# A static order for every engine, LN transposes by DMA and a denser attention: two layers of local attention and FFN on one core

## The chip, the cores and the metric

One core of one Trainium2 chip. The time is the device time of one execution in microseconds (us), as the median of several executions. The program runs on one core, so there is no second die to compare with; all runs told here are in the fast state. Each ratio is to runs of the kernel before on the same chip in the same rounds. Differences between two versions ("above the changed kernel") cross rounds and chips; the kernel before had medians of 1329.9 to 1330.6 us in them, so a microsecond between two versions is not read as a gain or a loss.

## The reference, cut to what matters

```python
# x: (1, 2048, 1024) bf16; 32 heads of 32; window 8, dilation 2; FFN width 3584
def _A_ref(x, wqkv, wo):
    q, k, v = ...                       # x @ wqkv, per head
    idx = pos[:, None] - (jnp.arange(8) * 2)[None, :]
    logits = einsum("bhsd,bhswd->bhsw", q, k[idx]) * scale   # masked where idx < 0
    o = einsum("bhsw,bhswd->bhsd", softmax(logits), v[idx])
    return o.reshape(B, S, D) @ wo

def _B_ref(x, w1, b1, w2, b2):
    r = relu(x @ w1 + b1)
    return (r * r) @ w2 + b2

x = A_x
for _ in range(2):                      # written out twice in the reference
    x = x + _A_ref(_layernorm(x), A_wqkv, A_wo)
    x = x + _B_ref(_layernorm(x), B_w1, B_b1, B_w2, B_b2)
```

## The kernel before

The work is cut into 8 units (2 layers x 4 blocks of 512 rows). A unit has these stages: SA (layernorm of the input and its transposition to channels on partitions), SQ (the q, k and v projections: `pq`), S2 (local attention, mostly on DVE), SW (the output projection `py`, residual, second layernorm and transposition), SF (the FFN: `ph` up, `py` down). Generators for the stages are advanced in turn so that a unit's attention runs on DVE while TensorE (PE) does another unit's FFN; a scheduler then orders the instructions by automatic priorities.

A layernormed tile of 128 rows is transposed by eight PE transposes through PSUM:

```python
def ln_transpose(self, xt, xnT, tl, dve_stats=False, evac_act=False):
    xn = self.xp.tile([128, D], BF, name="xn", tag="xn")          # pool of 2
    # ... mean and variance by two ACT passes over the tile (bn_stats on DVE where dve_stats)
    nc.scalar.activation(out=xn[:], in_=xt, func=ACTF.Identity, bias=nmr[:], scale=rstd[:])
    pt = self.ps_t.tile([128, self.KD, 128], BF, name="pt", tag="pt")
    for kd in range(self.KD):
        nc.tensor.transpose(pt[:, kd, :], xn[:, kd * 128:(kd + 1) * 128], self.ident[:])
    # ... copied to xnT by DVE or ACT
```

Attention: products `P` on DVE, summed in a tree of depth 2; a matmul of 32 columns for each window position gives logits by rows; softmax there; probabilities are transposed back by PE (`ptp`) and weight the values on DVE.

```python
for w in range(W):                                                # logits: lg
    for i, Pp in enumerate(d["finals"]):
        nc.tensor.matmul(lg[:, tl2, w, :], Pp[:, w, tl2*128:(tl2+1)*128], self.ind[:], ...)
# ... max, subtract, exp, sum, reciprocal, multiply
for w in range(W):                                                # back: ptp
    nc.tensor.transpose(ptp[:, w, :], p4[:, tl2, w].rearrange("p h r -> p (h r)"), self.ident[:])
# ... for every c: multiply with the v window, then three adds (8 -> 4 -> 2 -> 1 positions)
```

The order of the stages and the weights that are loaded ahead follow one list:

```python
for u in range(NU):
    if u + 1 < NU: prim.append(('SQa', u + 1))      # k, q
    prim.append(('SW', u))
    if u + 1 < NU: prim.append(('SQb', u + 1))      # v
    prim.append(('SF', u))                          # in two halves of the FFN width
```

## Time and profile before

| | before |
|---|---|
| time, median of the first 4 runs (of all 12) | 1330.5 us (1330.6) |
| span of the profiled run, granted clock | 1328.5 us, 0.996 |
| first `pq`; first `ph` | 16.93; 135.45 us |
| steady period of a unit | 161.1 us |
| DMA | 223.69 MB, 168 GB/s |

The page, the steady period and its matmuls are shown in the prediction. What it tells of the end in words only is PE's timeline where the last unit's SW stands alone. Columns here and in all timelines: start and duration in us, engine, line, operation, output<-inputs, shapes, count, and in brackets the idle time before it and what ended it.

```profile
1203.36 7.50 PE L457 MATMUL py<-wt,oT 128*128 128x512 bf16 x33
...
1217.48 0.62 PE L193 MATMUL pt<-ident,xn 128*128 128x128 bf16 x8 [0.20 <-ACT xn L190]
...
1221.44 0.62 PE L193 MATMUL pt<-ident,xn 128*128 128x128 bf16 x8 [2.91 <-ACT xn L190]
1224.70 1.03 PE L193 MATMUL pt<-ident,xn 128*128 128x128 bf16 x8 [2.64 <-ACT xn L190]
1226.56 8.61 PE L485 MATMUL ph<-xnT,wt 128*128 128x512 bf16 x31 [0.82 <-DVE xnT L198]
```

The reader is to see that from 1203.36 to 1226.56 PE has only this stage to do, that it waits for the layernorm result `xn`, 2.91 and 2.64 us for the last two tiles, and that the up projection cannot begin before the last tile is transposed.

### The profile page before, as it was taken

What the parts mean: (1) busy time and instruction counts of PE and PEld (TensorE: products, weight loads), DVE (VectorE), ACT (ScalarE), POOL (GpSimd) and SP (SyncE); (2) the same over time, 40 slices, a digit from 0 to 9 for tenths busy, and PEclk for the clock granted to TensorE, in tenths of its full rate; (3) what the DMA queues carried; (4) which work ended last, traced back from release to release, by engine and by line L of the source; (5) the groups of instructions that cost most, each with busy time, mean ns of one, the idle gap of its engine ahead of it and who ended that gap; (6) DMA issues with size and microseconds to landing.
All of it is one profiled execution on the core that took longest, in us unless ns stands there. A gap on an engine that the chain in (4) does not pass through costs nothing.

```text
span 1328.5 us, 17261 instructions
## 1 busy us (share of the span) xinstructions
PE 1285.2 (97%) x6972; PEld 679.8 (51%) x7104; DVE 830.1 (62%) x1170; ACT 681.1 (51%) x1229; POOL 2.9 (0%) x9
## 2 busy tenths in 40 slices
PE   6999999999999999999999999999999999997998
PEld 3665444654446544455445554455544555443443
DVE  4599993394935949268582777719676197926011
ACT  4647826287342964239561494615836166142622
POOL 0000000000000000000000000000000000000000
PEclk9999999999999999999999999999999999999999
DMA  8435544646355554656456464456644564446341
GB/s 214 160 127 158 175 141 146 205 159 201 126 196 185 180 175 143 200 189 206 123 174 235 160 221 152 135 188 212 200 127 163 195 214 131 130 150 223 127 135 56
DMA packets 180847, 223.69 MB, mean 168 GB/s; under 512 B 8608, under 2 KB 143776, under 8 KB 180768
## 3 DMA queue, kind: packets, MB, share of 16 engines
q1 hardware_dynamic: 177168, 222.58, 50.8%
q0 software_dynamic: 3600, 0.01, 0.4%
q8 instruction: 55, 0.90, 0.3%
q14 instruction: 24, 0.20, 0.0%
HBM read 209.98 MB, written 12.58 MB: 168 GB/s over the span
## 4 chain that ended last, share of the span: by engine, by line
PE 73%; DVE 14%; ACT 11%; issue 1%; DMA 0%; SPq 0%; ACTq 0%
PE py L506 29%; PE ph L485 28%; PE pq L268 12%; DVE P L316 5%; DVE P L335 4%; ACT xn L190 3%; ACT xn L181 3%; ACT xn L185 2%; PE pt L193 1%; DVE pr L411 1%; PE py L457 1%; PE ptp L398 1%; DVE xm L459 1%; ACT vT L270 1%; PE lg L362 1%
## 5 line engine op out<-in xcount | busy, mean ns | idle before, releaser
L485 PE MATMUL ph<-xnT,wt 128*128 128x512 bf16 x1751 | 393.2, 380 | 3.0 <-DVE xnT L198 0.8
L506 PE MATMUL py<-wt,r2t 128*128 128x512 bf16 x1753 | 389.4, 379 | 2.1
L268 PE MATMUL pq<-xnT,wt 128*128 128x512 bf16 x1500 | 341.0, 381 | 3.0 <-DVE xnT L198 0.8
L506 PEld LDWEIGHTS <-r2t 128*128 128x128 bf16 x1792 | 174.5, 98 | 207.1 <-ACT r2t L490 0.4
L485 PEld LDWEIGHTS <-wt 128*128 128x128 bf16 x1792 | 174.2, 98 | 206.7 <-issue 3.1
L268 PEld LDWEIGHTS <-wt 128*128 128x128 bf16 x1536 | 216.8, 144 | 107.5 <-issue 3.7
L489 ACT ACTIVATE r<-ph,b1T 128x512 bf16<-128x512 f32 x224 | 152.9, 683 | 98.3 <-PE ph L485 96.9
L411 DVE TENSOR_TENSOR pr<-pb,vT 128x2048 bf16<-128x2048 bf16 x128 | 156.1, 1235 | 44.2 <-ACT pb L399 44.2
L316 DVE TENSOR_TENSOR P<-qT,kT 128x2048 bf16<-128x2048 bf16 x128 | 153.7, 1226 | 37.0 <-ACT qT L270 37.0
L490 ACT ACTIVATE r2t<-r 128x512 bf16<-128x512 bf16 x224 | 140.7, 629 | 5.5
L270 ACT CAST kT<-pq 128x512 bf16<-128x512 f32 x64 | 37.6, 587 | 189.3 <-PE pq L268 189.3
L457 PE MATMUL py<-wt,oT 128*128 128x512 bf16 x496 | 114.0, 383 | 0.8
L335 DVE TENSOR_TENSOR P<-P 128x2048 bf16<-128x2048 bf16 x84 | 102.5, 1221 | 0.4
L412 DVE TENSOR_TENSOR pr<-pr 128x1024 bf16<-128x1024 bf16 x128 | 87.4, 698 | 0.0
L516 DVE TENSOR_TENSOR xo<-py,xm 128x512 bf16<-128x512 f32 x32 | 22.1, 692 | 101.9 <-PE py L506 100.0
L399 ACT COPY pb<-ptp 128x1024 bf16<-128x1024 bf16 x32 | 31.6, 1013 | 104.1 <-PE ptp L398 103.9
L457 PEld LDWEIGHTS <-oT 128*128 128x128 bf16 x512 | 50.1, 99 | 59.0 <-issue 2.4
L512 DVE TENSOR_TENSOR xm<-py,xm 128x512 f32<-128x512 f32 x64 | 44.4, 693 | 52.2 <-PE py L506 49.4
L270 ACT CAST qT<-pq 128x512 bf16<-128x512 f32 x64 | 37.5, 586 | 65.3 <-PE pq L268 65.3
L193 PE MATMUL pt<-ident,xn 128*128 128x128 bf16 x512 | 41.5, 227 | 29.5 <-ACT xn L190 28.7
L521 DVE TENSOR_TENSOR xof<-py,xm 128x512 f32<-128x512 f32 x32 | 22.1, 692 | 76.5 <-PE py L506 59.5
L193 PEld LDWEIGHTS <-xn 128*128 128x128 bf16 x512 | 32.4, 101 | 51.4 <-ACT xn L190 45.5
(61 smaller groups left out, 737.4 us busy)
## 6 DMA issues: line engine op xcount, KB each, us to landing
wt<-in_B_w_dram SPq DMA_DIRECT2D x88, 1024.0 KB, 6.0
wt<-in_A_wqkv_dram SPq DMA_DIRECT2D x48, 1024.0 KB, 6.0
wt<-in_B_w_dram SPq DMA_DIRECT2D x32, 768.0 KB, 4.5
wt<-in_A_wo_dram SPq DMA_DIRECT2D x16, 1024.0 KB, 6.2
xt<-xs SPq DMA_DIRECT2D x32, 512.0 KB, 4.4
xt<-in_A_x_dram SPq DMA_DIRECT2D x32, 256.0 KB, 3.7
xs<-xof SPq DMA_DIRECT2D x32, 256.0 KB, 3.1
out_dram<-xo SPq DMA_DIRECT2D x32, 128.0 KB, 2.0
```

What stands on the lines that cost most here:

```text
L193: nc.tensor.transpose(pt[:, kd, :], xn[:, kd * 128:(kd + 1) * 128], self.ident[:])
L268: nc.tensor.matmul(pq[:], fetch(nm)[kd // 4][:, kd % 4, c0:D:8], xnT[:, kd, :], start=(kd == 0), stop=(kd == KD - 1))
L270: nc.scalar.copy(dst[:, c0, off:off + BLK], pq[:])
L316: pi = nc.vector.tensor_tensor(P[:], qT[:, c, None, hb * HB:(hb + 1) * HB].to_broadcast([128, W, HB]), _win_ap(kT[:, c, :], HALO + hb * HB ...
L335: nc.vector.tensor_tensor(other[:], other[:], cur[:], ALU.add)
L411: nc.vector.tensor_tensor(pr[:], pb[:], vwin, ALU.mult)
L412: nc.vector.tensor_tensor(pr[:, 0:4, :], pr[:, 0:4, :], pr[:, 4:8, :], ALU.add)
L457: nc.tensor.matmul(py[:], oT[:, c, tl * 128:(tl + 1) * 128], wos[db][:, c, :], start=(c == 0), stop=(c == NCH - 1))
L485: nc.tensor.matmul(ph[:], wt[:, kd, cc * 128:(cc + 1) * 128], xnT[:, kd, :], start=(kd == 0), stop=(kd == KD - 1))
L489: nc.scalar.activation(out=r[:], in_=ph[:], func=ACTF.Relu, bias=self.b1T[:, f_idx:f_idx + 1], scale=1.0)
L490: nc.scalar.activation(out=r2t[:], in_=r[:], func=ACTF.Square)
L506: nc.tensor.matmul(py[:], r2[kf][:, tl * 128:(tl + 1) * 128], w2s[gi][:, j, :], start=(kf == 0), stop=(kf == KFH - 1))
```

## The change

Its intent: take work and waits away from PE, the engine that sets the time. The two files differ nearly everywhere; the core of the diff, with cuts marked:

```diff
+MM = 0.2157                      # estimated us of one matmul, used by the planner
+class Plan:                      # list scheduler: every operation has an engine, an
+    ...                          # estimated duration, a priority, what it reads and writes
+    def schedule(self): ...      # simulates the engines; the order found is the order emitted
-        self.wp = ctx.enter_context(tc.tile_pool(name="wp", bufs=5))
-        ...                      # one pool for each kind of buffer
+        p.caps.update(w=5, xt=2, P=5, pr=2, dn=1, pb=2, xm=8, xnA=1, xnB=1, xn=2, ...)
@@ layernorm
-        pt = self.ps_t.tile([128, self.KD, 128], BF, name="pt", tag="pt")
-        for kd in range(self.KD):
-            nc.tensor.transpose(pt[:, kd, :], xn[:, kd * 128:(kd + 1) * 128], self.ident[:])
+            nc.scalar.dma_start(scr(), xn[:])                 # to DRAM, issued by ACT
+            nc.sync.dma_start_transpose(xnT[:, tl], scr())    # back, transposed, issued by SP
@@ attention: logits replicated over the 4 partitions of a head, 512 columns at a time
-                        nc.tensor.matmul(lg[:, tl2, w, :], Pp[:, w, ...], self.ind[:], ...)
+                            nc.tensor.matmul(lg[j][:], self.grp[:]..., cur[:, 2 * j:2 * j + 2, :], ...)
+                nc.scalar.activation(out=e[:, 2*j:2*j+2, :], in_=lg[:], func=ACTF.Exp, scale=self.scale)
+                nc.vector.reciprocal(out=ri[:], in_=t[:, 0, :])         # 128 x 256
+                nc.vector.tensor_tensor(pb[:], e[:], ri[:, None, :].to_broadcast(...), ALU.mult)
-                    nc.tensor.transpose(ptp[:, w, :], p4[:, tl2, w]..., self.ident[:])
@@ build
+            if u + 1 < NU:
+                ...                                  # SA, k, SW(u), q, v of u + 1
+                self.S2(u + 1, 3)                    # tree of depth 3 (0 in unit 0)
+            self.SF1(u)
+            if u == NU - 2:
+                self.SW(u + 1)                       # last unit's SW before SF2 of the unit ahead
+            self.SF2(u)                              # down projection in one pass over 28 tiles
+        with self.tc.manual_schedule():
+            self.p.emit(self.place)
```

Besides: attention in fp16; the layernorm statistics of SW by `bn_stats` on DVE; the load of `b2b` from the SP queue to the GpSimd queue.

> **What bounds the kernel now.** I read the page first (busy table, chain that ended last), then what TensorE waited for, then a table of busy time by stretch, and last the timeline of PE alone, which gives the true cost of each kind of instruction.
>
> ```profile
> span 1328.5 us, 17261 instructions
> PE 1285.2 (97%) x6972; PEld 679.8 (51%) x7104; DVE 830.1 (62%) x1170; ACT 681.1 (51%) x1229; POOL 2.9 (0%) x9
> ...
> PE 73%; DVE 14%; ACT 11%; issue 1%; DMA 0%; SPq 0%; ACTq 0%
> ...
> PE pt L193 <- ACT xn L190: 28.7, 28, 10.1
> ```
>
> The reader is to see that PE is the bound and hardly ever waits for long: 28.7 us behind the layernorm (LN) output `xn`, 11.9 of them before the first projection. But 97% is not 97% useful: a matmul is recorded at 380 ns, while matmuls follow each other much faster, so short waits are hidden inside the records. The pace must be read from starts. By stretch, the middle of the kernel repeats with a period of 161.1 us (there are 8 units of 512 rows: 2 layers x 4 blocks):
>
> ```profile
> 722.00:883.10 161.10, 158.74 (x849) 84.13 (x864) 104.52 (x144) 85.66 (x158) 0.00 (x0) 1.00 0.54 178
> 883.10:1044.30 161.20, 158.84 (x850) 84.18 (x865) 104.90 (x145) 85.69 (x158) 0.00 (x0) 1.00 0.53 177
> ```
>
> Columns: length, then busy us of PE, weight load, DVE, ACT, POOL, then granted clock, DMA share, GB/s. DVE and ACT are busy 65% and 53% of a period, DMA 54%: none is near its limit. The timeline of PE in such a period:
>
> ```profile
> 721.82 27.79 PE L268 MATMUL pq<-xnT,wt 128*128 128x512 bf16 x126
> 749.45 9.66 PE L457 MATMUL py<-wt,oT 128*128 128x512 bf16 x43
> ...
> 775.62 0.62 PE L193 MATMUL pt<-ident,xn 128*128 128x128 bf16 x8
> 776.08 3.41 PE L268 MATMUL pq<-xnT,wt 128*128 128x512 bf16 x15
> ...
> 797.43 0.95 PE L362 MATMUL lg<-ind,P 128*128 128x32 bf16 x32
> 798.24 10.52 PE L485 MATMUL ph<-xnT,wt 128*128 128x512 bf16 x47
> 808.59 1.06 PE L398 MATMUL ptp<-ident,p 128*128 128x128 bf16 x16
> 809.49 1.89 PE L485 MATMUL ph<-xnT,wt 128*128 128x512 bf16 x7
> ```
>
> Start to start: the 128 projection matmuls (two records missing) take 749.45 - 721.82 = 27.63 us, 0.2159 each; a later run of 96 FFN matmuls takes 20.72 us. I use 0.2158 us. Eight LN transposes cost 0.46 us, 32 logit matmuls of 32 columns 0.81, 16 probability transposes 0.90; in the first unit 16 streamed logit matmuls cost about 0.41.
>
> **The sum before.** 5632 full matmuls (1536 pq, 512 wo, 1792 ph, 1792 FFN-down) x 0.2158 = 1215.4. Start to the first pq 16.9. Small PE work after it: 60 groups of LN transposes x 0.46 = 27.6, 16 x 0.90 = 14.4, 14 x 0.81 = 11.3, 16 x 0.41 = 6.6, together 59.9. Tail after the last matmul 3.6 (one 0.69 us add, one store). Sum 1295.8. The remaining 32.7 us are waits and slow clock: 28.7 - 11.9 = 16.8 recorded waits for `xn`; about 4 of slow clock (the first 34 pq take 9.90 us where 7.5 are due, 128 ph at 1226.6 take 29.2 where 27.6 are due); about 12 of short waits inside the records. A large part lies in 1203 to 1227, where the last unit's output projection and LN stand alone: 23 us for 13.8 us of matmuls and 1.8 of transposes.
>
> **What the Trainium skill says.** "TensorE: Matmul & The Clock Gate", section "Wait — 56ns, not 53.3ns?": back-to-back matmuls go at N / 2.4 GHz + 2.5 ns, 215.7 ns at N = 512 and 55.6 at N = 128, with a floor near 25 ns for small N. The trace agrees: 215.8 ns, 0.90/16 = 56 ns, 0.81/32 = 25 ns. So a 512-column logit matmul costs 8.5 times a 32-column one, and it pays only if far fewer are needed. The same page, section "What's actually happening": the array idles down to half clock after about 3.4 us without work and needs as long to recover; the trace agrees, pq at the start are 0.43 us apart before they drop to 0.2158. "DMA: Bandwidth & Descriptors", section "Latency and other measured facts", gives a DMA transpose 261 GB/s in a strided case; an estimate from that page is 1.0 us for 256 KB. No run here shows a DMA transpose yet.
>
> **The change, part by part.**
>
> Static order. The round-robin of generators and the automatic priorities go; a list scheduler inside the kernel fixes every engine's order. PE's emitted order, which can be read without running, is 712 full matmuls per unit: 64 k, 64 output projection, 120 q and v, 4 logits, 8 v, 224 up with 4 logits among them, 224 down.
>
> LN transposes. Only the first unit's eight stay on PE (four before the first pq, four after). The other 56 tiles are stored by ACT to DRAM and read back by transposing DMAs. PE: 56 x 0.46 = 25.8 us less. DVE loses the evacuation (0.69 each). Added: 56 x 256 KB written and read, 29 MB on 223.7, hence about 198 GB/s against 168.
>
> Attention on PE. The logits are summed per head and replicated by one 128x128 matrix, 512 columns a time: 8 per unit in units 1 to 7, 64 in unit 0: 120 x 0.2158 = 25.9 us. Removed: all probability transposes and 32-column logits, 14.4 + 11.3 + 6.6 = 32.3. Net -6.4.
>
> DVE per unit. Removed: max, subtract, sum, reciprocal, weighting (2 x 2.97 + 4 x 1.22 = 10.8), evacuations 5.5, the half-sum adds 8 x 0.69 = 5.5. Added: two tree adds 2.4; two denominators, estimated from the f32 rows (1.22 + 0.69 + 0.43, plus up to 2.0 for a 256-wide reciprocal scaled from 0.55 at 64) 8.7; two f32 weightings of 2048, estimated at 2.3 each, 4.6; LN statistics 8 x 0.69 + 1.4 = 6.9. Balance +0.8: about 105 of a 153.6 us period. ACT loses two 1.1 us passes per output-projection tile and the probability copies, gains 64 exponentials of about 0.63: it goes to about 590 us.
>
> Last unit. Its output projection now comes after the up projection of unit 6 and inside its down projection; the last up projection starts 133 matmuls (28.7 us) after the last of it. The isolated stretch at 1203 should vanish: 7.9 us of waits and 1.5 of slow clock.
>
> Sum: start 16.9 + 5752 x 0.2158 = 1241.3 + four transpose groups 1.8 + tail 3.6 + slow clock at the start 2.4 = 1266.0 of span if PE never waits. For waits I choose 8: 3 in unit 0, where the DVE chain (16 products, two normalisations, 16 weighted sums of 2.28 us) ends at about 110 us, when PE wants its second half; 1 for the first DMA transposes; 0.5 in each of five steady periods; 1.5 around the split projection. Span 1274, and the timed median is 2.0 above the span: 1276, ratio 0.959. Nearly all of it is PE work and PE waits taken away: per steady period 161.1 - 153.6 = 7.5 us, which is 4.5 of transposes and logits and about 2.1 of LN waits, rest rounding.
>
> **The rivals.**
> (a) The DMA round trip of LN becomes the wait. Store, landing, transpose, landing; 256 KB lands in 3.1 to 3.7 us now, so about 7 us plus 4 of LN. For it: SP issues weights and transposes in one queue, so a late transpose holds back weights behind it. Against: after the last output projection of a unit PE has 128 matmuls (27.6 us) before `ph` needs the result, and weights run up to five tiles (about 7 us of PE each) ahead. It needs transposes of over 8 us each to bite; then 1300 to 1340.
> (b) DVE becomes the bound in places: attention must be done in about 138 us from the first q to the next output projection, and has about 105 us of work in it. It can bite in unit 0 and in the split projection of unit 7: 1280 to 1290.
> (c) A static order made from estimated durations is brittle: any engine in strict order that runs late stops others, with no reordering. For it: the before kernel's order adapts no better on the chip, but had slack. It would show as 2 to 4 us of waits in each of 7 periods: 1290 to 1300.
> (d) The waits vanish altogether: 1268.
>
> **Range and chances.** The floor is firm (counts times a measured pace), 1266 + 2 = 1268, with perhaps 2 us of play at the start. So low 1266. Above, (b) and (c) reach 1296. Only (a) in its bad form exceeds the 1304 that still counts as 2% faster; I give that 10%, and 2% of it to a loss.
>
> **What would show it.** The steady period should be 153.6 to 155 us, no `ptp`, 64 `pt`, 120 logit matmuls at 0.216; first `ph` between 132 and 139 us (now 135.5, so unit 0 gains nothing); no gap before the last `ph`; DVE busy 64 to 70%, ACT 45 to 48%; transposes landing in under 5 us. Wrong if PE shows waits for the transposed tiles or for weights, if the 512-column matmul with a strided moving operand (four runs of 128) goes slower than 0.2158, or if the logit matmuls in fp16 do.

## The result, and the profile after

| | before | after |
|---|---|---|
| time, median | 1330.62 us (1329.7 to 1331.17, 12 runs) | 1276.14 us (1275.27 to 1277.52, 8 runs) |
| span, clock | 1328.5, 0.996 | 1273.2, 0.997 |
| first `pq`; first `ph` | 16.93; 135.45 | 14.31; 138.71 |
| steady period | 161.1 | 153.67 |
| DVE / ACT busy | 62% / 51% | 69% / 48% |
| DMA | 223.69 MB | 252.91 MB, 199 GB/s |

The ratio is 0.9592, 95% interval 0.9583 to 0.9602. Ratios are the mean time of one kernel's fast runs over that of the other's of the same rounds, so not quite the ratio of the medians quoted.

The page after: span, busy time and the chain that ended last.

```profile
span 1273.2 us, 14846 instructions
...
PE 1249.3 (98%) x5761; PEld 638.1 (50%) x5816; DVE 880.9 (69%) x1170; ACT 606.1 (48%) x1065; POOL 4.1 (0%) x10
...
PE 93%; DVE 5%; DMA 1%; issue 1%; SPq 0%; ACT 0%; DVEq 0%
```

PE went from 6972 recorded instructions to 5761, and its share of the chain from 73% to 93%: what ends last is now a row of matmuls and little else. What PE waited for (us in total, times, longest):

```profile
PE pt L387 <- ACT xn L377: 9.3, 3, 8.2
PE py L574 <- DVE o L543: 5.2, 3, 2.3
PE pq L451 <- DMA w<-in_A_wqkv_dram: 1.2, 1, 1.2
```

The 28.7 us behind `xn` are now 9.3, all at the start, and the transposed tiles `xnA` and `xnB` are not in this list with a DMA at all. The largest new wait is 5.2 us for `o`, the attention output of unit 0. A steady period as a window (length, busy us of PE, weight load, DVE, ACT, POOL, clock, DMA share, GB/s), then PE in one period:

```profile
390.80:544.50 153.70, 153.33 (x707) 78.51 (x713) 110.78 (x144) 76.42 (x136) 0.00 (x0) 1.00 0.67 213
```

```profile
237.13 13.98 PE L451 MATMUL pq<-xnA,w 128*128 128x512 bf16 x64
250.94 13.98 PE L574 MATMUL py<-w,o 128*128 128x512 bf16 x62
264.76 26.06 PE L451 MATMUL pq<-xnA,w 128*128 128x512 bf16 x120
290.66 1.03 PE L497 MATMUL lg<-P,grp 128*128 128x512 f16 x4
...
293.25 15.70 PE L602 MATMUL ph<-xnB,w 128*128 128x512 bf16 x72
```

From one period to the next the matmuls move by 153.67 us, as 712 x 0.2158 = 153.65 would have it. There is no transpose in the period. From the end of the output projection at 264.76 to the first `ph` at 293.25 there are 28.5 us of `pq` and logits, in which the layernorm round trip lies. The end of the kernel:

```profile
1110.82 7.07 PE L574 MATMUL py<-w,o 128*128 128x512 bf16 x31
...
1137.37 7.07 PE L574 MATMUL py<-w,o 128*128 128x512 bf16 x31
...
1172.98 48.51 PE L602 MATMUL ph<-xnB,w 128*128 128x512 bf16 x224
```

The last unit's SW stands in two parts, at 1110.82 and 1137.37, inside the down projection of the unit ahead, and the last `ph` follows at 1172.98 with no wait in brackets. The 23 us of the kernel before are gone.

Where the 55.3 us of span went: the first `pq` is 2.6 us earlier; from there to the first `ph` unit 0 takes 5.9 us longer; from the first `ph` to the last matmul's end it is 1131.1 us against 1189.5, 58.4 less; the tail is 0.2 shorter. Of the 5.9 us of unit 0, 3.6 are PE work by count: 64 logit matmuls of 512 columns (13.8 us) stand where 16 groups of small logits and two of probability transposes took 8.4, and four groups of layernorm transposes (1.8) are gone. So the denser logits cost unit 0 5.4 us, and gain 1.7 in each of the other seven. The other 2.3 us are waits and slow clock.

### The profile page after: what moved, and what is told of

It reads as the page before. It is cut to its first block, busy times and chain, and to the rows that moved or that the text cites. A ratio compares the mean times of both kernels' runs of the same rounds, so it can differ in the third digit from the quotient of the medians.

```text
span 1273.2 us, 14846 instructions
## 1 busy us (share of the span) xinstructions
PE 1249.3 (98%) x5761; PEld 638.1 (50%) x5816; DVE 880.9 (69%) x1170; ACT 606.1 (48%) x1065; POOL 4.1 (0%) x10
## 2 busy tenths in 40 slices
DMA packets 247974, 252.91 MB, mean 199 GB/s; under 512 B 68640, under 2 KB 203808, under 8 KB 247904
## 4 chain that ended last, share of the span: by engine, by line
PE 93%; DVE 5%; DMA 1%; issue 1%; SPq 0%; ACT 0%; DVEq 0%
PE ph L602 30%; PE py L628 30%; PE pq L451 22%; PE py L574 8%; DVE pr L538 1%; PE lg L497 1%; DMA w<-in_A_wqkv_dram 1%; DVE pr L541 1%; DVE P L482 1%; DVE pr L542 1%; SPq L282 0%; DVE o L543 0%; DVE pb L528 0%; DVE dn L522 0%; DVE ri L525 0%
## 5 line engine op out<-in xcount | busy, mean ns | idle before, releaser
L602 PE MATMUL ph<-xnB,w 128*128 128x512 bf16 x1792 | 389.4, 379 | 0.0
L628 PE MATMUL py<-w,r 128*128 128x512 bf16 x1753 | 386.2, 379 | 2.1
L451 PE MATMUL pq<-xnA,w 128*128 128x512 bf16 x1536 | 339.2, 381 | 2.0 <-DMA w<-in_A_wqkv_dram 1.2
L628 PEld LDWEIGHTS <-r 128*128 128x128 bf16 x1792 | 175.4, 98 | 211.4
L602 PEld LDWEIGHTS <-w 128*128 128x128 bf16 x1792 | 175.3, 98 | 211.1
L451 PEld LDWEIGHTS <-w 128*128 128x128 bf16 x1536 | 220.4, 144 | 115.9 <-issue 3.0
L638 DVE TENSOR_TENSOR xo<-py,xm 128x512 f32<-128x512 f32 (+1 forms) x64 | 44.1, 691 | 236.5 <-PE py L628 236.4
L482 DVE TENSOR_TENSOR P<-q,k 128x2048 f16<-128x2048 f16 x128 | 151.3, 1224 | 24.5 <-ACT q L453 24.5
L538 DVE TENSOR_TENSOR pr<-pb,v 128x2048 f16<-128x2048 f16 x128 | 156.6, 1224 | 0.8
L608 ACT ACTIVATE r<-r 128x512 bf16<-128x512 bf16 x224 | 141.3, 631 | 7.0
L490 DVE TENSOR_TENSOR P<-P 128x2048 f16<-128x2048 f16 x98 | 120.0, 1225 | 2.8
L574 PE MATMUL py<-w,o 128*128 128x512 bf16 x496 | 113.3, 382 | 6.2 <-DVE o L543 5.2
L579 DVE TENSOR_TENSOR xm<-py,xt 128x512 f32<-128x512 f32 x64 | 43.6, 689 | 12.7 <-PE py L574 12.1
```

The lines of the kernel that those rows point to most:

```text
L451: nc.tensor.matmul(pq[:], wv[:, kd % 4, c0:D:8], xnT[:, :, kd, :], start=(kd == 0), stop=(kd == KD - 1))
L482: nc.vector.tensor_tensor(cur[:], q[:, c, None, hb * HB:(hb + 1) * HB].to_broadcast([128, W, HB]), _win_ap(k[:, c, :], HALO + hb * HB, HB) ...
L490: nc.vector.tensor_tensor(other[:], other[:], cur[:], ALU.add)
L538: nc.vector.tensor_tensor(pr[:], pb[:], _win_ap(v[:, c, :], HALO + hb * HB, HB), ALU.mult)
L574: nc.tensor.matmul(py[:], o[:, c, tl * 128:(tl + 1) * 128], wos[db][:, c, :], start=(c == 0), stop=(c == NCH - 1))
L602: nc.tensor.matmul(ph[:], wt[:, kd, cc * 128:(cc + 1) * 128], xnT[:, :, kd, :], start=(kd == 0), stop=(kd == KD - 1))
```

## The experiments

Every kernel below gave a correct result. The theory on trial: PE is the bound throughout, so time moves as PE work and PE waits do, and the order keeps the DMA round trip hidden. The main rival: PE was no tight bound, or DMA latency and the order's own brittleness would show.

**1. The transposes back on PE** (`a_pt_pe`), all else as changed.

```diff
-                        (("xnd", 2 * layer, t), 0), 20.0, False)
+                        (("xnd", 2 * layer, t), 0), 20.0, False, on_pe=True)
-                    (("xnd", 2 * layer + 1, t), 0), 1.0, True, on_pe=(u == 0))
+                    (("xnd", 2 * layer + 1, t), 0), 1.0, True, on_pe=True)
```

> The changed kernel with the LN transposes of all units back on PE, all else (static order, new logits, moved last projection) kept. Counting theory: 56 groups of 8 transposes at 0.46 us come back on the bound engine and nothing else changes, 1276 + 25.8 = 1302 us, with the steady period going from 153.7 to 157.3. Rival, the waits for the LN output were the gain: they come back too (some 2 us a unit, 17 in all), 1315 to 1320. Rival, the static order was the gain and transposes cost little: under 1288.

Measured 1306.54 us (1305.31 to 1307.56), ratio 0.9822 [0.9807, 0.9837]: 30.4 above the changed kernel. The same stage begins at 247.14 and 404.40, a period of 157.26 us, so 3.6 us in each of seven units are the transposes (8 x 0.46 = 3.7); about 5 more are lost in unit 0, whose first `ph` comes at 146.93. More telling is what remains: with the same transposes on PE as before, the period is 157.26 and not 161.1. Of those 3.8 us, 1.7 are the attention's PE work (by count). The other 2.1 are no PE work: after unit 0 no wait for `xn` is left. The order is the likely cause, but the second layernorm's statistics, moved to DVE, and the buffers changed with it and were not tried alone.

**2. A shallower tree** (`a_depth2`): 8 more logit matmuls in each of seven units, less DVE work.

```diff
-                self.S2(u + 1, 3)
+                self.S2(u + 1, 2)
```

> The changed kernel with a logit tree of two levels in place of three in units 1 to 7: two groups of 512-column logit matmuls per half instead of one, one tree add less on DVE per half. Counting theory: 7 units x 8 more matmuls x 0.2158 = 12.1 us slower, 1288, though DVE does 14 adds (about 16 us) less. Rival, DVE sets the pace somewhere in a period (it is 72% busy there): no slower than 1278, or faster.

Measured 1288.01 us (1287.79 to 1289.01), ratio 0.9686: 11.9 above the changed kernel, where 56 x 0.2158 = 12.1 are due. The period is 155.4 us, 1.73 longer. PE work is paid in full, and the DVE time that this version saves buys nothing. PE is the bound.

**3. The last unit's SW after the down projection again** (`a_last_sw`).

```diff
-            if u == NU - 2:
-                self.SW(u + 1)
+            if u == NU - 1:
+                self.SW(u)          # ahead of SF1(u)
```

> The changed kernel with the last unit's output projection after the down projection of the unit before, as in the kernel before, not inside it. Counting theory plus latency: the whole LN round trip (add, statistics, normalise about 4 us, store about 4, transposing load about 4, part of it beside the projection's last tiles) stands alone on the path, plus about 2 us of slow clock: 10 to 16 us slower, 1286 to 1292. Rival, the lone stretch cost little: under 1280.

Measured 1291.84 us (1289.83 to 1294.44), ratio 0.9713: 15.7 above. PE at that place:

```profile
1159.71 13.98 PE L574 MATMUL py<-w,o 128*128 128x512 bf16 x64
1185.78 6.43 PE L602 MATMUL ph<-xnB,w 128*128 128x512 bf16 x20 [12.10 <-DMA xnB<-xnd1B]
```

With nothing to cover it, the layernorm round trip through DRAM leaves PE idle for 12.1 us after the last output projection. Its place in the order was worth all of these 15.7 us.

**4. The DMA transposes in the kernel before, nothing else** (`b_dma_t`), from unit 1 on.

```diff
+        if scr is not None:
+            nc.scalar.dma_start(scr, xn[:])
+            nc.sync.dma_start_transpose(xnT[:, :, tl * 128:(tl + 1) * 128], scr)
+            return
         pt = self.ps_t.tile([128, self.KD, 128], BF, name="pt", tag="pt")
```

> The kernel before with one part of the change alone: LN transposes by DMA (store, transposing load) in all but unit 0; its own order, logits and layout kept. Counting theory: 25.8 us of PE work go, but its order leaves only 64 projection matmuls (13.8 us) and the logits between the last output projection and the first up projection, and the last unit's projection stands alone with a round trip about 8 us longer than the PE way: net about 10 to 18 us faster than 1330.6, 1313 to 1321. Rival, the round trip is hidden in any order: 1297 to 1305. Rival, it is exposed in every unit: slower than 1330.

Measured 1383.4 us (1381.38 to 1387.22), ratio 1.0404 [1.0384, 1.0423], clock 0.966. A miss: slower by 53 us, while PE has 25.8 us less to do (56 tiles at 0.46). The period is 169.2 us. The transposition by DMA is thus not a gain by itself. ACT waited long for its own stores to free `xn`, of which there are two buffers, so the first suspicion was those buffers.

**5. The same with four `xn` buffers** (`b_dma_t_xn4`).

```diff
-        xn = self.xp.tile([128, D], BF, name="xn", tag="xn")
+        xn = self.xp.tile([128, D], BF, name="xn", tag="xn", bufs=4)
```

> b_dma_t (the kernel before with LN transposes by DMA alone) was 53 us slower, not 10 to 18 faster. Its trace shows ACT waiting for a store to free one of only two xn tiles, 36 us in all, and PE waiting behind. Here the xn pool has four tiles, as large as the one of the changed kernel. Theory, the tile held by the store was the new wait: most of the loss goes, 1325 to 1345. Rival, the order is the cause (64 matmuls between output and up projection are too few for the round trip): still over 1360.

Measured 1385.69 us (1383.8 to 1392.25), ratio 1.0427: the theory of the buffers fell. PE, where the output projection of unit 1 ends and where `ph` begins:

```profile
277.79 4.91 PE L463 MATMUL py<-wt,oT 128*128 128x512 bf16 x22
...
309.94 0.61 PE L492 MATMUL ph<-xnT,wt 128*128 128x512 bf16 x1 [0.89 <-DMA xnT<-xnd0B]
```

From 282.54, where the next matmuls begin, to 309.94 are 27.4 us, with about 17 us of work between; in the trace PE also stands 7.4 us behind `ptp` there, but the last tile `xnT` landed only just ahead of 309.94, so `ph` could not have gone earlier. Why so late? ACT in that stretch:

```profile
297.06 1.06 ACT L182 ACTIVATE xn<-xt 128x1024 bf16<-128x1024 bf16 x1 [3.09 <-DMA xt<-in_A_x_dram]
...
301.45 0.34 ACTq L193 DMA_DIRECT2D xnd0B<-xn  x1
```

The last residual add of this SW was done at 284.8. Its normalised tile was stored at 301.45, because ACT's order had placed passes over the next unit's `xt` tiles in between, and one of those waited 3.09 us for its load. Then 8.5 us for store, landing, transposing load and landing. In the changed kernel the same add is done at 265.65 and the store issued at 270.23: 4.6 us on ACT and not 16.7. So in this stretch it is ACT's order, more than the DMA, that makes the tile late. This is read from the two traces; the order alone was not exchanged in the kernel before. Nor is it all of the loss: over the whole run PE's largest wait is the one for the probabilities (`ptp` behind DVE's `p`), 42.2 us in six places, and what delays those was not followed to its end.

**6. Weighted sums of unit 0 by pairs of chunks** (`a_pair0`). In unit 0 DVE's chain ended at 117.9 us and not at about 110, and PE waited for it. In the kernel before two chunks alternate:

```profile
74.36 2.37 DVE L411 TENSOR_TENSOR pr<-pb,vT 128x2048 bf16<-128x2048 bf16 x2
...
78.91 2.37 DVE L411 TENSOR_TENSOR pr<-pb,vT 128x2048 bf16<-128x2048 bf16 x2
```

Two chunks begin every 4.55 us, 2.28 for one. In the changed kernel each add directly follows the instruction whose result it reads:

```profile
68.59 1.23 DVE L538 TENSOR_TENSOR pr<-pb,v 128x2048 f16<-128x2048 f16 x1
69.86 0.69 DVE L541 TENSOR_TENSOR pr<-pr 128x1024 f16<-128x1024 f16 x1
...
71.26 1.22 DVE L538 TENSOR_TENSOR pr<-pb,v 128x2048 f16<-128x2048 f16 x1
```

That is 71.26 - 68.59 = 2.67 us for one chunk (2.65 for the next). The edit:

```diff
+        def av_pairs(hb):            # two chunks: mult, mult, add, add, add, add, add, add
+            for c in range(0, NCH, 2):
+                ...
+                p.add("DVE", 4.56, fp, ...)
-        av(0)
+        (av_pairs if u == 0 else av)(0)      # and for av(1)
```

> The changed kernel with the weighted sums of unit 0 issued two chunks at a time, so that no DVE add directly follows the instruction whose result it reads; same instructions, same count. In the changed kernel a chunk takes 2.65 us start to start there, in the kernel before (paired) 2.28. Theory, dependence between neighbours costs DVE about 0.1 us per instruction and this delayed unit 0: chunk pitch 2.28, the DVE chain ends about 6 us earlier, and PE, which lost 7.3 us around the first output projection, gains 4 to 6: 1270 to 1272. Rival, fp16 operands make DVE slower than bf16: pitch stays at 2.65, 1276. Rival, PE waits there for something else: pitch 2.28 but 1275 to 1276.

Measured 1275.34 us (1274.7 to 1276.01), ratio 0.9588 [0.9575, 0.9601]: the same as the changed kernel. On DVE the theory held: pairs go every 4.56 us (73.40, 77.96, 82.52) and the chain ends at 112.2. For PE it gained nothing:

```profile
118.21 0.83 PE L346 MATMUL pt<-ident,xn 128*128 128x128 bf16 x8 [3.85 <-ACT xn L305]
...
138.97 3.40 PE L619 MATMUL ph<-xnB,w 128*128 128x512 bf16 x15
```

With DVE earlier, the planner moved a transpose of the second layernorm forward, and PE now waits for ACT's `xn`. The first `ph` is at 138.97, where it was 138.71.

**7. As 6, with unit 0's transposes ranked later** (`a_pair0_pt3`).

```diff
-            p.add("PE", 0.46, t1, [(xn, 0)], [(pt, 0), (xnT, ("t", tl))], -5.0, name="pt")
+            p.add("PE", 0.46, t1, [(xn, 0)], [(pt, 0), (xnT, ("t", tl))], self.nxt() + 16, name="pt")
```

> a_pair0 ended DVE's chain of unit 0 5.75 us earlier and won nothing, because the planner then put the first LN transposes of unit 0 on PE before the last 16 output-projection matmuls, where PE waited 3.85 us for the normalised tile. Here the same, with those transposes given a later rank, so that they stand after the projection and one v group; nothing else is changed. Theory, place in PE's strict order was what ate the gain: first up projection at 134 to 136 us (138.7 in the changed kernel), 1271 to 1273, the fastest version. Rival, something else keeps PE there: 1275 to 1276 again.

Measured 1277.16 us (1276.62 to 1278.08), ratio 0.9603. A miss; the wait moved once more:

```profile
138.32 4.00 PE L619 MATMUL ph<-xnB,w 128*128 128x512 bf16 x9 [5.03 <-DVE xnB L348]
```

DVE had a bias add and two tree adds ahead of the last two copies to `xnB`.

**8. As 6, with the next unit's `x` loads after the first weights** (`a_pair0_xlate`), against the 1.25 us that PE waits for q weights at the start.

```diff
-            x, xv = self.load_x(layer, t, after, tag=...)
+            x, xv = self.load_x(layer, t, after, prio=9.5 if u == 1 else None, tag=...)
```

> As a_pair0, and the x tiles of the second unit are loaded after the first k and q weights and not before them. Theory: the wait for the q weights at 22 us (1.25 recorded, with hidden parts and a slower clock perhaps 2) goes, 1 to 2 us faster than a_pair0, 1268 to 1271: the fastest of all. Rival: the first LN of unit 1 then comes late and holds casts in ACT's strict order, no gain or a loss.

Measured 1275.98 us (1275.23 to 1276.58), ratio 0.9591: no gain. The wait for weights is now 1.84 us, at 20.63.

**9. The `b2b` load back at the head of the SP queue** (`a_b2b_sp`).

```diff
-        nc.gpsimd.dma_start(self.b2b[:], ...)
+        nc.sync.dma_start(self.b2b[:], ...)
```

> The changed kernel with the broadcast load of the bias b2 put back at the head of SP's queue, where the kernel before has it. The first projection began at 14.31 us in place of 16.93, which the prediction did not foresee. Theory, the 256 KB bias load ahead of the x tiles delayed them: first statistics from 3.5 back to about 6 us, first pq at 16.5 to 17, but the k and q weights are on the path a few us later in any case, so 0.5 to 2.5 us slower in all, 1276.5 to 1278.5. Rival, the early start comes from the new order of the statistics on DVE: first pq stays below 15.

Measured 1276.61 us (1276.46 to 1277.6), ratio 0.96. The first `pq` is at 16.57, so the bias load ahead of `x` does cost 2.3 us at the start; but then the weights are there when PE wants them, the first `ph` is at 139.83, and little of the 2.3 us reaches the end.

**10. Store and transposing load both twice** (`a_dma_twice`), to see how much of the round trip is hidden.

```diff
             nc.scalar.dma_start(scr(), xn[:])
+            nc.scalar.dma_start(scr(), xn[:])
             nc.sync.dma_start_transpose(xnT[:, tl], scr())
+            nc.sync.dma_start_transpose(xnT[:, tl], scr())
```

> The changed kernel with every LN store and every transposing load done twice, one after the other: the round trip gets about 7 us longer and 29 MB more move. Theory, the round trip lies wholly under 28 us of q and v projections or the two FFN stages, and DMA is near 65% busy: 0 to 2 us slower, 1276 to 1278. Rival, it is nearly exposed, or SP's one queue holds back weights: 10 us or more slower, with PE waits for the transposed tile or for weights.

Measured 1410.39 us (1401.45 to 1412.11), ratio 1.0589, clock 0.968. A miss, and a confounded test, as an ACT line shows:

```profile
307.29 1.56 ACT L455 CAST q<-pq 128x512 f16<-128x512 f32 x3 [4.20 <-DMA xnd0B<-xn]
```

The second store overwrites what the first wrote and so waits for it, and ACT's compute stands behind that wait: this cast of `q` began 4.20 us late. The run says nothing on the round trip.

**11. Only the transposing load twice** (`a_tr_twice`), on SP, which does no compute.

```diff
             nc.sync.dma_start_transpose(xnT[:, tl], scr())
+            nc.sync.dma_start_transpose(xnT[:, tl], scr())
```

> a_dma_twice did not test what it was meant to: ACT, in its strict order, waited 3 to 5 us before each second store for the first one to land, and its casts came late. Here only the transposing load is done twice, by SP. Theory, the round trip has slack and SP's queue has too: 0 to 3 us slower, 1276 to 1279. Rival, SP's queue is nearly full: each second transpose waits 3.5 us for the first, 56 of them hold back weights, 10 us or more slower with PE waiting for weights or xnB.

Measured 1321.19 us (1319.94 to 1326.07), ratio 0.9945 [0.9924, 0.9966]: 45 us above the changed kernel, another miss. What SP, ACT and PE waited for, a line of each:

```profile
SPq L354 <- DMA xnB<-xnd1B: 58.0, 16, 9.1
```

```profile
ACT xn L330 <- DMA xt<-xs: 44.1, 4, 13.6
```

```profile
PE ph L603 <- ACT v L454: 20.6, 3, 7.0
...
PE pq L452 <- DMA xnA<-xnd0A: 8.1, 1, 8.1
```

The second load of a tile waits about 3.6 us for the first (58.0 us over 16), with everything behind it in SP's queue. Among that are the `xt` loads of the next unit; ACT, in strict order, waits for them 44.1 us in 4 places (in the changed kernel ACT has no such wait), its casts of `v` come late, and PE's `ph` waits behind those. The transposed tile itself was late twice: `pq` of unit 1 waited 8.1 us for `xnA`, and `ph` once 1.6 us for `xnB`. So most of what PE waited for seems to have come through the held queue. This is the rival's size, but by the `xt` loads: for weights PE waited 0.2 us. And the test is confounded as experiment 10 was: SP is held because the second load waits for the first, while in the changed kernel SP waits for no transposing load to land. A single load that takes longer was not tried.

**12. A wrong duration in the planner** (`a_mm380`): the 0.380 us at which a matmul is recorded, in place of its pace.

```diff
-MM = 0.2157
+MM = 0.380
```

> The changed kernel with one constant of its planner wrong: a matmul is taken to last 0.380 us (the duration of a record) and not 0.2157. Same instructions, another fixed order: the logits now stand after 88 projection matmuls (19 us) and 40 more (8.6 us), while DVE needs about 17 us per half for the products and the tree. Theory, a static order is only as good as its durations: PE waits about 8 us per steady unit on the logits, the array cools, 1315 to 1345. Rival, order matters little since PE is full anyway: under 1285.

Measured 1488.24 us (1485.9 to 1490.25), ratio 1.1188 [1.1172, 1.1203]. The direction was expected, the size was not. One wait of the kind that costs most (14 of them, the longest 28.9 us):

```profile
348.25 1.89 PE L497 MATMUL lg<-P,grp 128*128 128x512 f16 x4 [17.12 <-DVE P L490]
```

PE waits 168.7 us in all for tree sums. The planner believed that PE had time, put layernorm passes between ACT's casts of `q`, and DVE's products waited for the casts. One constant, with no change of any instruction's work, costs 212 us.

## Why the prediction was right

The predicted 1276 was met by 1276.14. That PE's work and pace decide the time was right; that the sum fits to a microsecond is luck, as errors of 2 to 5 us cancel in it. By its steps:

- **The sum of PE work.** Right. 5752 matmuls at 0.2158 us are 1241.3 us, and from the first `ph` on PE loses 0.3 us in 1131.1: 5240 matmuls in that time are 0.2159 each. The strided moving operand and the fp16 logits go at this pace too (four logit matmuls from 290.66 to 291.52 in the full timeline). Experiment 2 shows that each matmul counts.
- **What each part is worth.** Undone singly, the transposes give back 30.4 us (25.8 are their PE work by count; most of the rest is lost in unit 0, where the planner made another order) and the place of the last SW 15.7. The 6.4 us of attention work are counted, not undone. These three come to 52.5 of 54.5; undone parts need not add up, and unit 0's loss is among them. Two of the prediction's own sums are off, without effect on its total: "4.5 of transposes and logits" per period is 3.7 + 1.7 = 5.4, which with 2.1 of waits is the whole 7.5, and the "7.9 us of waits" of the last SW are 7.6 between the lines shown (1203.36 to 1226.56 less 13.8 and 1.8).
- **The waits.** Right in sum, wrong in its terms, and the errors cancelled. The start was 14.3 and not 16.9 (2.6 less): the prediction left out that `b2b` leaves the SP queue, which experiment 9 shows. "3 in unit 0" was too small: 7.3 us were lost from 101.95 to 138.71. Of these, 5.4 are recorded waits, and most of the rest is slow clock, which the prediction put only at the start: the granted clock was 0.51 from 114 to 121 us and 1.00 before and after. No wait there is longer than 2.26 us; the prediction had quoted about 3.4 us without work, and the trace agrees on the half pace but not on that length as one piece. The term that was mis-sized is "16 weighted sums of 2.28 us", which took 2.65, so that the chain ended at 117.9 and not 110. The other five allowed for DMA transposes, steady periods and the split projection came to 0.3. At the start, slow clock and short waits (weights 1.25, logits 0.9) took 4.8 where 2.4 were put down.
- **What limits unit 0** stays open. Three versions (the changed kernel, experiments 6 and 7) reach the first `ph` at 138.7, 139.0 and 138.3 us, each with other waits before it. PE's own work to that point is 112.3 us by count (512 matmuls and four groups of transposes from 14.31 on), so 12.1 us of waits and slow clock are left to explain. The DVE chain was a part of it, as PE's lines in the changed kernel show, but making it shorter gained nothing:

```profile
112.68 0.39 PE L574 MATMUL py<-w,o 128*128 128x512 bf16 x1 [0.85 <-DVE o L543]
115.32 0.61 PE L574 MATMUL py<-w,o 128*128 128x512 bf16 x1 [2.26 <-DVE o L543]
117.98 1.89 PE L574 MATMUL py<-w,o 128*128 128x512 bf16 x4 [2.05 <-DVE o L543]
...
138.71 17.43 PE L602 MATMUL ph<-xnB,w 128*128 128x512 bf16 x80
```

- **Rival (a), the round trip as the wait.** It did not come, as predicted, but its reason was thin. The store and the transposing load of such a tile (KB, us from issue to landing):

```profile
xnd1B<-xn ACTq DMA_DIRECT2D x16, 256.0 KB, 3.7
...
xnB<-xnd1B SPq DMA_TRANSPOSE x16, 3.9
```

  Both are under 5 us, and the cover of 28.5 us suffices. Whether "it needs transposes of over 8 us each to bite" holds is not shown: no run has one slow load. Experiment 11 shows another way for it to bite, by 45 us: holding SP's queue for about 3 us per tile (178.5 us in all 56), which the prediction named only for weights and which came through the `xt` loads and ACT.
- **Rival (c), a brittle order.** Right that it did not show with these durations; but experiments 10 to 12 show how little it takes. And the same transposes in the kernel before lose 53 us (experiment 4), where the prediction's count would have given a gain: it had put the transposes and the order side by side as two gains. That the first needs the second is the likely reading, not shown apart from the other changes.
- **Sizes.** DVE was busy 111 us of a period, not 105 (the chunks of the weighted sums, 16 at 2.65 us and not 2.28, would account for 5.9 of it); the wide reciprocal 1753 ns (up to 2.0 us estimated) and the weighting 2.29 us (2.3). All are off the path in steady state.

## What to carry to other kernels

Where one engine is the bound, count its instructions by their start-to-start pace, and ask of every transfer that replaces work on it whether the order leaves it cover: here the same DMA transposes cost 53 us in the kernel before and save 30 in the changed one, most likely by the order. A static order is as good as its durations, and these must be paces, not recorded lengths. Before removing the last wait in a stretch, look which wait stands behind it: three versions of unit 0 reached its first `ph` within 0.7 us of each other.

## What the Trainium skill lacked or had wrong

- "DMA: Bandwidth & Descriptors", section "Latency and other measured facts", has a bandwidth for the DMA transpose but no time from issue to landing. Here a 256 KB transposing load landed after 3.3 to 4.0 us, against an estimate of 1.0 us from that page's 261 GB/s, and the bare layernorm round trip through DRAM left PE idle for 12.1 us.
- The same page, section "Anatomy of one DMA — SWDGE (gpsimd) path", says that a DMA's semaphore wait happens on the issuing sequencer. The runs agree, but the page doesn't say what it costs where the issuer is a compute engine: a cast and an activation on ACT stood 4.20 and 7.07 us behind stores (experiment 10).
- "VectorE: DVE Perf Modes", section "The DRAIN you can't avoid", reports eight copies that take as long with semaphores between as without. It has no figure for a chain in which each instruction reads the one before: here such a chunk of four took 2.65 us, and 2.28 where two chunks alternate, about 0.12 us for each of three dependent steps. The trace doesn't tell whether the result or a wait makes the difference.
- No page that I found has the reciprocal's time: 128 x 64 f32 took 549 ns, 128 x 256 took 1753 ns, on DVE.
